# Experts 1 to 7 in the order of their token counts, with 384 down to 256 columns by rank, and hi and lo side by side in short tails

## The chip, the cores and the metric

The kernel runs on one core of a Trainium2 chip. The metric is the time of one execution on the device, in microseconds (us); of several executions the median counts. The engines run side by side and wait for each other by semaphores: PE (TensorE) multiplies matrices, ACT (ScalarE) and DVE (VectorE) work on vectors, POOL (GpSimd) does small work and issues gathers and scatters, and SP (SyncE) issues the other transfers. Each engine takes its instructions in the order of its own queue.

## What is computed

Three blocks follow one another on 4 x 576 = 2304 tokens of width 512: an attention with a decay bias, a gated MLP with a product over the sequence, and at the end a mixture of 8 experts, which is what the change touches:

```
logits = x @ w_gate                       # [B, S, 8]
local_gate = sigmoid(x @ w_local)
for b: for s:                             # in order, since e may be that of the token before
    e = argmax(logits[b, s]) if s == 0 or local_gate[b, s] < 0.5 else prev_e
    out[b, s] = softmax(logits[b, s])[e] * (relu(x[b, s] @ w1[e]) @ w2[e])
```

`w1[e]` is 512 x 1024 and `w2[e]` 1024 x 512. Each token goes to one expert. With the inputs as they are drawn, the reference sends 227, 356, 289, 239, 277, 278, 294 and 344 tokens to experts 0 to 7.

## The kernel before

All large products run as three matmuls in `fp32r`: a value is split in a rounded part (hi) and the rest (lo), and hi x hi, hi x lo and lo x hi are summed in PSUM (`mm3`). So every operand of the experts exists twice, side by side in one tile.

The routing of each of the four batches (`route`) is done with small matmuls and DVE work on one-hot tables; it leaves in `tbl` (of the last batch in `ids`) the token numbers, one column of 128 for each block of 128 tokens of an expert, and in `carry` the counts. The batches' MLP runs in `M_steps` and `O_steps`; the last batch's routing falls between the output products of that batch and the first layer of expert 0.

Then `experts` runs the experts one by one, in the order 0 to 7. Each has room for `CAP` = 3 blocks of 128 tokens, 384 columns, whatever its count; free places hold a token number out of range, which the gathers and scatters skip. Expert 0 is started early and in parts (`early_L1`, `L1_rows`). For an expert e of 1 to 7 the code is:

- `gather(e + 1)`: three indirect transfers on POOL, each 128 rows of the next expert, into one of two buffers `xgs`;
- `L1`: 8 column blocks f of the first layer, each 4 x 3 matmuls with a stationary block of w1 and the moving tokens `xT` (384 columns), then ReLU on ACT and the rest (lo) on DVE, into `hT`;
- `next_w(e + 1, ...)` for w1 and `new_xT(e + 1)`: 12 transposes on PE, then copies to `xT`;
- `L2` for three token blocks t: 8 x 3 matmuls with a stationary block of `hT` (128 tokens) and 512 moving columns of w2, then a scaled copy to `y` on ACT and an indirect scatter to `out` on POOL;
- `next_w(e + 1, ...)` for w2.

`load_w` brings one of the 8 pieces of an expert's weights (512 KB) by SP into `wraw` (2 buffers); ACT rounds it to hi and DVE computes lo, into one of 10 buffers `wp`. The buffers come free in a ring, so the loads of the next expert run behind the matmuls of this one. After the eighth expert `overflow` repeats the work for any token block beyond the third of an expert, in a loop over a list made on the chip (`emit_olist`); with the counts above the list is empty.

A scheduler sets the order of the instructions on each engine, from the order of the code and its own estimates.

Of the kernel before, what the change touches and what calls it, by code (L numbers as in the profile page):

```python
# [33 lines left out]
def kernel(  # L34
# [42 lines left out]
    def dma(out, in_):  # L77
        return SP.dma_start(out=raw(out), in_=raw(in_))
# [66 lines left out]
    NOV = NT // 128 - CAP  # L145
    NL = E * (NBLK - CAP)
    olist = T(const, [1, 2 * NOV + 1], I32, "olist")
    ids_d = dram.tile([128, NC], I32, name="ids_d")

# [126 lines left out]
    def emit_consts2():  # L276
        POOL.iota(io8, pattern=[[1, 8]], base=0, channel_multiplier=0)
        it = T(mp, [128, 512], I32, "ga", bufs=2)
        POOL.iota(it[:, 0:8], pattern=[[-1, 8]], base=8, channel_multiplier=0)
        POOL.iota(it[:, 8:8 + NQ], pattern=[[1024, NQ]], base=9, channel_multiplier=8)  # L280
        POOL.iota(it[:, 16:17], pattern=[[0, 1]], base=0, channel_multiplier=1)
        POOL.iota(it[:, 32:160], pattern=[[1, 128]], base=0, channel_multiplier=0)
        POOL.iota(it[:, 160:160 + NC], pattern=[[1, NC]], base=0, channel_multiplier=0)
        POOL.iota(it[:, 320:320 + B * NQ], pattern=[[-S, B], [-128, NQ]], base=FREE, channel_multiplier=-1)
        DVE.tensor_copy(out=w8d, in_=it[:, 0:8])
        DVE.tensor_copy(out=s8, in_=it[:, 8:8 + NQ])
# [11 lines left out]
        POOL.memset(onesb, 1.0)  # L298
        POOL.memset(onesf, 1.0)
# [558 lines left out]
    def route(b, lt):  # L858
# [85 lines left out]
        a = DVE.tensor_tensor(out=ids if b == B - 1 else tbl, in0=tbl, in1=pt[:, NC:2 * NC], op=ALU.subtract)  # L944
        for i in range(NQ):
            DVE.tensor_tensor(out=carry[0:QM[i]], in0=carry[0:QM[i]], in1=oh[0:QM[i], i, :], op=ALU.add)
        dmarks.append(a)

        ex = T(rp, [128, NQ, E], F32, "ex")
        DVE.tensor_tensor(out=ex, in0=l8, in1=mxb, op=ALU.subtract)  # L950
# [12 lines left out]
        dma(x2_d[r0:r0 + 512, DM:ROW].rearrange("(i p) c -> p i c", p=128), ps4[:, 0:NQ - 1])  # L963
        dma(x2_d[r0 + 512:r0 + S, DM:ROW], ps4[0:S - 512, NQ - 1])

    def emit_olist(pool, after):

        nb = NBLK - CAP
# [4 lines left out]
        x = POOL.iota(li[0:1, 0:NL], pattern=[[0, E], [128, nb]], base=128 * CAP, channel_multiplier=0)  # L973
        behind(x, after)
        POOL.iota(li[0:1, 128:128 + NL], pattern=[[1, E], [0, nb]], base=0, channel_multiplier=0)
        POOL.iota(li[0:1, 256:256 + NL], pattern=[[NBLK, E], [1, nb]], base=CAP, channel_multiplier=0)
        for a in range(3):
            DVE.tensor_copy(out=lf[0:1, 128 * a:128 * a + NL], in_=li[0:1, 128 * a:128 * a + NL])
        cx = T(pool, [128, 2, E, nb], BF16, "cx")
        behind(DVE.tensor_copy(out=cx[:, 0], in_=carry.unsqueeze(2).to_broadcast([128, E, nb])), dmarks[-1].ins.name)  # L980
        DVE.tensor_copy(out=cx[:, 1], in_=pad.unsqueeze(2).to_broadcast([128, E, nb]))
# [19 lines left out]
    def overflow():  # L1001
        of = out.rearrange("b s d -> (b s) d")
        n_ov = nc.values_load(olist[0:1, 2 * NOV:2 * NOV + 1], min_val=0, max_val=NOV)  # L1003
        with tc.For_i(0, n_ov) as it, tc.tile_pool(name="ov", bufs=1, side="left") as op:
            e = nc.sync.value_load(olist[0:1, bass.ds(it, 1)], min_val=0, max_val=E - 1)
            c = nc.sync.value_load(olist[0:1, bass.ds(it + NOV, 1)], min_val=CAP, max_val=NC - 1)
# [45 lines left out]
            )  # L1052


    WP = {}

    def load_w(e, j):

        r = T(wpool, [128, 1024], F32, "wraw", bufs=2)
        if j < KD:  # L1060
            dma(r, w1[e, 128 * j:128 * j + 128, :])
        else:
            f0 = 256 * (j - KD)
            x = dma(r.rearrange("p (a d) -> p a d", a=2), w2[e, f0:f0 + 256, :].rearrange("(a p) d -> p a d", p=128))
# [29 lines left out]
    def xT(xt, xg, n0, n):  # L1094

        w = 128 * n
        for kt in range(KD):
            pt = ps()
            for blk in range(n):
                PE.transpose(pt[:, 128 * blk:128 * blk + 128], xg[:, n0 + blk, 128 * kt:128 * kt + 128], ident)  # L1100
            ACT.copy(out=xt[:, 0, kt, 0:w], in_=pt[:, 0:w])
            DVE.tensor_tensor(out=xt[:, 1, kt, 0:w], in0=pt[:, 0:w], in1=f32v(xt[:, 0, kt, 0:w]), op=ALU.subtract)

    def L1(e, xt, ht, w_, after={}):
        for f in range(NF):
# [24 lines left out]

# [26 lines left out]
    def L1_rows(pool, e, xt, ht):  # L1157
# [11 lines left out]
        for z in range(2):  # L1169
# [14 lines left out]
    def experts(pool):  # L1184
        xts = {}

        def new_xT(e, n0=0):
            xts[e] = T(pool, [128, 2, KD, CC], F32R, "xT", bufs=2)
            xT(xts[e], xgs[e % 2], n0, CAP - n0)

        def new_hT():
            return T(pool, [128, 2, NF, CC], F32R, "hT", bufs=1)

        def early_L2(t):
            L2(pool, 0, early["ht"], t, early["xg"][:, t, DM:DM + 1], ids0[:, t:t + 1])
# [10 lines left out]
        for e in range(E):  # L1206
# [15 lines left out]
            for t in range(t0, CAP):  # L1222
                c = e * NBLK + t
                xg = xgs[e % 2][:, t] if e else early["xg2"]
                L2(pool, e, ht, t - t0, xg[:, DM:DM + 1], ids[:, c:c + 1])
# [151 lines left out]
```

## Time and profile before

| | us |
|---|---|
| median of 3 executions | 848.91 |
| lowest and highest | 845.52 and 854.72 |
| the profiled execution, its own time | 853.13 |
| its span, first to last instruction | 851.3 |
| PE busy in the span | 807.9 (95%) |
| DVE, ACT, POOL busy | 549.7, 463.2, 345.4 |

The span is what the profile's times count from; the profiled execution is 4.2 us slower than the median. In rows of the profile, a line names the kernel's line (L700 is the matmul in `mm3`), the engine, the operation, the tile written and those read, the shapes, and how many instructions stand together. For matmuls "128\*18" is the stationary block (rows x columns). Matmuls overlap, so a matmul's duration is longer than the distance from its start to that of the next; all prices below are distances between starts.

### The profile page before, as it was taken

How to read it: one execution, taken by the hardware profiler on the slowest of the kernel's cores; microseconds unless marked ns; L12 is line 12 of the kernel's file. 1: busy time of each engine (PE TensorE's matmuls, PEld its weight loads, DVE VectorE, ACT ScalarE, POOL GpSimd, SP SyncE). 2: the span in 40 equal slices, each digit the busy share in tenths (PEclk: the TensorE clock that was granted, in tenths of full speed). 3: DMA queues.
4: the chain of work that ended last, by engine and by line, in shares of the span. 5: the costliest groups of instructions: out<-in, count | busy, mean ns of one | idle time of the engine just before them, and what ended most of it. 6: DMA issues, size and time to landing. Idle time of an engine off the chain costs nothing. (4 is left out here: it accounts for less than half of the span.)

```text
span 851.3 us, 14839 instructions
## 1 busy us (share of the span) xinstructions
PE 807.9 (95%) x4803; PEld 684.5 (80%) x4803; DVE 549.7 (65%) x1567; ACT 463.2 (54%) x1070; POOL 345.4 (41%) x619
## 2 busy tenths in 40 slices
PE   8888999898999999999998899989999999999995
PEld 4555778687987988889888688778989989899894
DVE  7769669886677799968887467773545344353420
ACT  5756677785554788628785236134444344343410
POOL 3658754575551578724586002052021211313101
PEclk9977999998999999999999999999999999999998
DMA  7997799975477777679551673144564533545400
GB/s 159 220 225 219 163 230 282 290 188 105 104 166 216 176 157 198 144 182 259 112 169 41 209 249 121 38 129 152 180 191 133 184 129 124 194 132 182 124 4 35
DMA packets 119603, 138.69 MB, mean 163 GB/s; under 512 B 69494, under 2 KB 82934, under 8 KB 119524
## 3 DMA queue, kind: packets, MB, share of 16 engines
q1 hardware_dynamic: 115684, 128.23, 57.2%
q0 software_dynamic: 3840, 9.48, 3.0%
q8 instruction: 40, 0.66, 0.3%
q14 instruction: 39, 0.32, 0.1%
HBM read 90.96 MB, written 23.13 MB: 134 GB/s over the span
## 5 line engine op out<-in xcount | busy, mean ns | idle before, releaser
L1070 DVE TENSOR_TENSOR wp<-wraw,wp 128x1024 fp32r<-128x1024 f32 x63 | 76.6, 1224 | 102.8 <-ACT wp L1069 96.7
L700 PE MATMUL ps<-wp,hT 128*128 128x512 f32 x528 | 123.7, 393 | 0.0
L700 PE MATMUL ps<-xT,wp 128*128 128x384 f32 x672 | 119.7, 337 | 0.0
L700 PEld LDWEIGHTS ps<-xT,wp 128*128 128x128 f32 x672 | 117.8, 188 | 0.7
L1126 POOL DMA_INDIRECT out_dram<-y,ids x24 | 30.0, 1250 | 212.9 <-ACT y L1125 175.0
L700 PEld LDWEIGHTS ps<-wp,hT 128*128 128x128 f32 x528 | 98.6, 188 | 21.8
L414 POOL TENSOR_SCALAR E<-E,lsum 128x128 f32<-128x128 f32 (+4 forms) x160 | 97.6, 613 | 41.0 <-DVE lsum L411 28.9
L406 ACT ACTIVATE E<-E,negm 128x128 f32<-128x128 f32 (+4 forms) x160 | 96.7, 605 | 22.0 <-DVE negm L398 14.9
L1069 ACT CAST wp<-wraw 128x1024 fp32r<-128x1024 f32 x64 | 66.5, 1050 | 64.9 <-DMA wraw<-in_moe_w_dram 58.2
L700 PE MATMUL ps<-qk 128*128 128x128 f32 (+5 forms) x372 | 89.1, 337 | 6.1 <-DVE mv L759 2.8
L398 DVE CUSTOM_DVE_ANT_0 E<-ps,zmask 128x128 f32<-128x128 f32 (+4 forms) x160 | 75.6, 474 | 23.1 <-PE ps L700 21.9
L410 POOL TENSOR_SCALAR lsum<-lsum 128x1 f32<-128x1 f32 (+1 forms) x160 | 39.9, 249 | 121.1 <-ACT E L406 112.9
L432 PE MATMUL ps<-ident,E 128*128 128x128 f32 (+1 forms) x480 | 75.8, 265 | 10.9 <-POOL E L414 5.2
L432 PEld LDWEIGHTS ps<-ident,E 128*128 128x128 f32 (+1 forms) x480 | 51.8, 141 | 25.4 <-POOL E L414 9.8
L700 PE MATMUL ps<-wsg,vg 128*128 128x288 f32 x448 | 70.2, 307 | 1.7 <-DVE etb L442 1.0
L700 PEld LDWEIGHTS ps<-qk 128*128 128x128 f32 (+2 forms) x372 | 54.4, 175 | 15.3 <-DVE mv L759 3.1
L700 PEld LDWEIGHTS ps<-wsg,vg 128*128 128x128 f32 x448 | 63.5, 194 | 3.7 <-DVE etb L442 1.3
L464 PE MATMUL ps<-etb,vv 128*128 128x320 f32 (+5 forms) x340 | 65.3, 345 | 0.4 <-DVE tst L330 0.3
L464 PEld LDWEIGHTS ps<-etb,vv 128*128 128x128 f32 (+1 forms) x340 | 50.5, 182 | 14.1 <-issue 7.0
L700 PE MATMUL ps<-xh,w 128*128 128x288 f32 x256 | 59.5, 311 | 0.0
L1114 DVE SCALAR_TENSOR_TENSOR hT<-ps,hT 128x384 fp32r<-128x384 f32 x56 | 30.2, 553 | 39.2 <-ACT hT L1113 39.2
L700 PE MATMUL ps<-w,vg 128*128 128x512 f32 (+1 forms) x216 | 54.7, 398 | 0.2 <-ACT stg L494 0.2
(291 smaller groups left out, 1604.4 us busy)
## 6 DMA issues: line engine op xcount, KB each, us to landing
wraw<-in_moe_w_dram SPq DMA_DIRECT2D x64, 512.0 KB
qk<-tst SPq DMA_DIRECT2D x28, 432.0 KB
w<-wv_d SPq DMA_DIRECT2D x16, 512.0 KB
w<-wo_d SPq DMA_DIRECT2D x16, 512.0 KB
qk<-tst SPq DMA_DIRECT2D x28, 288.0 KB
w<-wu_d SPq DMA_DIRECT2D x12, 512.0 KB
nq<-in_q_dram SPq DMA_DIRECT2D x16, 288.0 KB
nk<-in_k_dram SPq DMA_DIRECT2D x16, 288.0 KB
```

What stands on the lines that cost most here:

```text
L398: hred[g] = DVE.tensor_tensor_reduce(out=e[0:M, a:z], in0=pt[0:M, 0:n], in1=zmask[0:M, m0:m0 + n], scale=-1.0, scalar=BIG if hi == 0 else ...
L406: ACT.activation(out=e[0:M, 0:N], in_=e[0:M, 0:N], func=ACTF.Exp, scale=-1.0, bias=nm[0:M, last:last + 1], accum_out=l[0:M, i:i + 1])
L410: POOL.tensor_scalar(out=l[0:M, c], in0=l[0:M, c], scalar1=1e-9, scalar2=0.0, op0=ALU.add, op1=ALU.add)
L414: POOL.tensor_scalar(out=Et[g, x][0:M, 0:n], in0=Et[g, x][0:M, 0:n], scalar1=l[0:M, x:x + 1], scalar2=1.0, op0=ALU.mult, op1=ALU.mult)
L432: PE.transpose(pt[:, j * M:(j + 1) * M], e[0:M, 128 * j:128 * (j + 1)], ident[0:M, 0:M])
L464: PE.matmul(pt[0:128 if wide else 64, a:n], lhsT=l, rhs=et[0:kk, z, j, a:n] if g >= F4 else f32v(et[0:kk, 0, j, a:n]), start=(j == 0 and n ...
L700: ms = [PE.matmul(pt, lhsT=l, rhs=r, start=(first_ and x == 0), stop=(last_ and x == n - 1)) for x, (l, r) in enumerate(pairs)]
L1069: c = ACT.copy(out=w[:, 0, :], in_=r)
L1070: a = (POOL if (e, j) == (0, KD) else DVE).tensor_tensor(out=w[:, 1, :], in0=r, in1=f32v(w[:, 0, :]), op=ALU.subtract)
L1114: DVE.scalar_tensor_tensor(out=ht[:, 1, f, 0:w_], in0=pt[:, 0:w_], scalar=0.0, in1=f32v(ht[:, 0, f, 0:w_]), op0=ALU.max, op1=ALU.subtract)
L1126: POOL.indirect_dma_start(out=of[:, :], out_offset=bass.IndirectOffsetOnAxis(ap=idx, axis=0), in_=y, in_offset=None, bounds_check=NT - 1, ...
```

## The change

The counts of experts 1 to 7 are ranked on the chip after the last batch's routing (`rank`, on DVE, with one small matmul). The loop over e then means: the expert of rank e - 1. Its weights are loaded from an address that SP reads from the table `order`, its token numbers come from `idsr`, and its width is fixed in the code: `CAPS[e]` = 384, 352, 320, 320, 288, 288 and 256 columns. By rank the counts above are 356, 344, 294, 289, 278, 277 and 239. Expert 0 stays as it was.

For widths of 320 and 288 the third block has 64 or 32 tokens (n). There `hT` keeps hi and lo of these tokens next to one another (`hparts`), and `L2_tail` takes a stationary block of 2n columns against the hi half of w2 and one of n columns against the lo half: two matmuls for each f where there were three. The sums of rows 0 to n and n to 2n are added afterwards. For 352 the third block has 96 tokens and keeps the three matmuls, and for 256 there is none. `emit_olist` now compares a count with the width of its rank.

```diff
+    CAPS = [384, 384, 352, 320, 320, 288, 288, 256]
...
+    def rank():
+        pn = rs()
+        PE.matmul(pn[:, 0:E], lhsT=onesb, rhs=carry, start=True, stop=True)
+        key = T(rp, [128, E], F32, "key")
+        DVE.scalar_tensor_tensor(out=key, in0=pn[:, 0:E], scalar=8.0, in1=w8d, op0=ALU.mult, op1=ALU.add)
...
+        DVE.tensor_tensor(out=gt, in0=key[:, 1:E].unsqueeze(1).to_broadcast(sq), in1=key[:, 1:E].unsqueeze(2).to_broadcast(sq), op=ALU.is_gt)
+        DVE.tensor_reduce(out=rk, in_=gt, axis=AX.X, op=ALU.add)
...
+        DVE.tensor_copy(out=order, in_=rk[0:1])
...
+        DVE.tensor_copy(out=idsr, in_=ir)
...
     def load_w(e, j):
         r = T(wpool, [128, 1024], F32, "wraw", bufs=2)
+        if e and j == 0:
+            chosen[e] = nc.sync.value_load(order[0:1, e - 1:e], min_val=1, max_val=E - 1)
+        ee = bass.ds(chosen[e], 1) if e else slice(0, 1)
         if j < KD:
-            dma(r, w1[e, 128 * j:128 * j + 128, :])
+            dma(r, w1[ee, 128 * j:128 * j + 128, :].rearrange("o p f -> p (o f)"))
...
     def gather(e):
-        for blk in range(CAP):
-            c = e * NBLK + blk
-            x = fetch(xgs[e % 2][:, blk, :], ids[:, c:c + 1])
+        for blk in range((CAPS[e] + 127) // 128):
+            n = min(128, CAPS[e] - 128 * blk)
+            x = fetch(xgs[e % 2][0:n, blk, :], idsr[0:n, e - 1, blk:blk + 1])
...
+    def hparts(ht, w):
+        fl = ht.rearrange("p f z c -> p f (z c)")
+        def hi(f, a, z):
+            return fl[:, f, a:z]
+        def lo(f, a, z):
+            o = ht.shape[3] if w not in TAILS else w if a >= EC else 2 * w - EC
+            return fl[:, f, o + a - EC:o + z - EC] if w in TAILS and a >= EC else fl[:, f, o + a:o + z]
+        return hi, lo
...
+            for a, z in ((0, w_),) if w_ not in TAILS else ((0, EC), (EC, w_)):
+                DVE.scalar_tensor_tensor(out=lo(f, a, z), in0=pt[:, a:z], scalar=0.0, in1=f32v(hi(f, a, z)), op0=ALU.max, op1=ALU.subtract)
...
+    def L2_tail(pool, e, ht, xg, n):
...
+            for z in (0, 1) if f < NF - 1 else (1, 0):
+                m = n if z else 2 * n
+                PE.matmul(pt[0:m, :], lhsT=hi(f, EC, EC + m), rhs=w[:, z, :], start=(f == z == 0), stop=(f == NF - 1 and z == 0))
+        lo, y = [T(pool, [128, DM], F32, "y", bufs=3) for _ in range(2)]
+        ACT.copy(out=lo[0:n], in_=pt[n:2 * n])
+        DVE.tensor_tensor(out=lo[0:n], in0=pt[0:n], in1=lo[0:n], op=ALU.add)
+        ACT.activation(out=y[0:n], in_=lo[0:n], func=ACTF.Copy, scale=xg[0:n, DM:DM + 1])
...
             if e:
-                for _ in L1(e, xt, ht, CC):
+                for _ in L1(e, xt, ht, CAPS[e]):
```

Ahead of the last batch's routing the engines' queues stay as they were, but for eight small fills on POOL and one copy on DVE at the very start. Three places differ.

On DVE, the rows from the last table of token numbers to the first copies for expert 0's third block: before (`hTA` is the first layer's result of expert 0, `wp` its weights).

```order
L944 TENSOR_TENSOR ids_94<-tbl_92,rt 128x144
L1070 TENSOR_TENSOR wp_8070<-wraw_8068,wp_8070 128x1024
L980 COPY cx_8889<-carry_93 128x120
L1114 SCALAR_TENSOR_TENSOR hTA_7921<-ps,hTA_7921 128x256
L1070 TENSOR_TENSOR wp_8075<-wraw_8073,wp_8075 128x1024
L1114 SCALAR_TENSOR_TENSOR hTA_7921<-ps,hTA_7921 128x256 x2
L1070 TENSOR_TENSOR wp_8080<-wraw_8078,wp_8080 128x1024
L1114 SCALAR_TENSOR_TENSOR hTA_7921<-ps,hTA_7921 128x256 x2
L1070 TENSOR_TENSOR wp_8207<-wraw_8205,wp_8207 128x1024
L1102 TENSOR_TENSOR xT_8113<-ps,xT_8113 128x128 x4
```

The same place on DVE in the changed kernel, from the second weight piece on; `key` to `idsr` are the ranking's.

```order
L1118 TENSOR_TENSOR wp_8113<-wraw_8111,wp_8113 128x1024
L988 SCALAR_TENSOR_TENSOR key_7839<-rt,w8d_78 128x8
L1179 SCALAR_TENSOR_TENSOR hTA_7959<-ps,hTA_7959 128x256 x2
L991 TENSOR_TENSOR gtr_7841<-key_7839 128x49
L993 TENSOR_REDUCE rk_7843<-gtr_7841 128x7
L995 TENSOR_TENSOR hot_7845<-rk_7843,iof_95 128x49
L996 TENSOR_TENSOR gtr_7841<-hot_7845,iof_95 128x49
L1002 TENSOR_TENSOR im_7850<-hot_7845,tbl_92 128x7x7 x3
...
L1118 TENSOR_TENSOR wp_8118<-wraw_8116,wp_8118 128x1024
...
L998 CAST order_98<-rk_7843 1x7
L1179 SCALAR_TENSOR_TENSOR hTA_7959<-ps,hTA_7959 128x256
L1005 CAST idsr_99<-ir_7854 128x21
```

Some 15 small operations now stand between expert 0's last pieces of work, and the weight piece that followed them (`wp_8207`, expert 1's first) has moved behind the copies of `xT`.

On SP, the rows around the first weight load of the second expert: before, then now.

```order
L78 DMA wraw_8078<-in_moe_w_dram 128x2x512
L78 DMA wraw_8205<-in_moe_w_dram 128x1024
L78 DMA wraw_8210<-in_moe_w_dram 128x1024
L78 DMA wraw_8215<-in_moe_w_dram 128x1024
```

```order
L78 DMA wraw_8116<-in_moe_w_dram 128x2x512
L1106 TENSOR_LOAD order_98
L1106 ISA x2
L78 ISA
L78 DMA wraw_8243<-in_moe_w_dram 128x1024
L78 ISA
L78 DMA wraw_8257<-in_moe_w_dram 128x1024
L1106 TENSOR_LOAD order_98
L1106 ISA x2
```

The first load of the second expert now waits for `order`; the other six reads of `order` stand together behind the second load, and each later load has one address instruction ahead of it.

On PE, the third block of the second layer of the third expert after expert 0 (320 columns now), and the start of the next expert: before, then now.

```order
L700 MATMUL ps<-wp_8852,hT_8911 128x512 x6
L700 MATMUL ps<-wp_8857,hT_8911 128x512 x6
L700 MATMUL ps<-wp_8862,hT_8911 128x512 x6
L700 MATMUL ps<-wp_8867,hT_8911 128x512 x6
L700 MATMUL ps<-xT_9052,wp_9034 128x384 x3
```

```order
L1206 MATMUL ps<-wp_8917,hT_8977 128x512
L1206 MATMUL ps<-wp_8917,hT_8977 64x512
L1206 MATMUL ps<-wp_8917,hT_8977 128x512
L1206 MATMUL ps<-wp_8917,hT_8977 64x512
...
L1206 MATMUL ps<-wp_8932,hT_8977 128x512
L1206 MATMUL ps<-wp_8932,hT_8977 64x512 x2
L1206 MATMUL ps<-wp_8932,hT_8977 128x512
L713 MATMUL ps<-xT_9135,wp_9117 128x320 x3
```

The 24 matmuls of the tail are 16 now, with stationary blocks of 128 and 64 columns in turn, and the first layer that follows has 320 columns instead of 384.

## Rows read from the trace of the kernel before

**Rows 1.** Page, engines; then stretches: length, busy time by engine, PEclk, DMA share, GB/s.

```profile
PE 807.9 (95%) x4803; PEld 684.5 (80%) x4803; DVE 549.7 (65%) x1567; ACT 463.2 (54%) x1070; POOL 345.4 (41%) x619
...
600.00:650.00 50.00, 50.00 (x270) 46.84 (x269) 25.41 (x33) 24.55 (x38) 9.18 (x7) 1.00 0.56 171
```

**Rows 2.** Timeline of PE, experts 5 to 7: start, duration (us).

```profile
756.87 16.62 PE L700 MATMUL ps<-wp,hT 128*128 128x512 f32 x72
773.32 17.09 PE L700 MATMUL ps<-xT,wp 128*128 128x384 f32 x96
790.25 1.47 PE L1100 MATMUL ps<-ident,xg 128*128 128x128 f32 x12
791.48 16.82 PE L700 MATMUL ps<-wp,hT 128*128 128x512 f32 x72
808.14 16.83 PE L700 MATMUL ps<-xT,wp 128*128 128x384 f32 x96
824.81 16.97 PE L700 MATMUL ps<-wp,hT 128*128 128x512 f32 x72
```

**Rows 3.** Timeline of PE, last batch's MLP and expert 0's first layer.

```profile
529.75 6.68 PE L700 MATMUL ps<-wsg,vg 128*128 128x288 f32 x49
536.27 0.69 PE L700 MATMUL ps<-vg,wgl 128*18 128x288 f32 x4
536.80 0.85 PE L700 MATMUL ps<-w,vg 128*128 128x512 f32 x3
537.49 0.29 PE L700 MATMUL ps<-vg,wgl 128*18 128x288 f32 x1
537.62 0.63 PE L700 MATMUL ps<-w,vg 128*128 128x512 f32 x2
...
555.90 4.58 PE L700 MATMUL ps<-xTA,wp 128*128 128x256 f32 x36
560.32 0.42 PE L941 MATMUL rt<-aa,l 128*128 128x288 bf16 x2
```

**Rows 4.** Page, groups: second and first layer's matmuls and first layer's weight loads.

```profile
L700 PE MATMUL ps<-wp,hT 128*128 128x512 f32 x528 | 123.7, 393 | 0.0
L700 PEld LDWEIGHTS ps<-xT,wp 128*128 128x128 f32 x672 | 117.8, 188 | 0.7
```

**Rows 5.** Timeline of DVE: around the routing, and behind it.

```profile
548.43 0.20 DVE L878 TENSOR_REDUCE am<-eq 128x5 f32<-128x40 f32 x1
...
579.36 0.88 DVE L1102 TENSOR_TENSOR xT<-ps,xT 128x128 fp32r<-128x128 f32 x4 [3.46 <-ACT xT L1101]
588.44 2.36 DVE L1070 TENSOR_TENSOR wp<-wraw,wp 128x1024 fp32r<-128x1024 f32 x2 [8.20 <-ACT wp L1069]
```

**Rows 6.** Timelines of POOL and PE: first gather behind the routing, first use.

```profile
570.27 1.00 POOL L1083 DMA_INDIRECT xg<-x_d,ids  x1 [0.16 <-POOL xg L1342]
...
591.51 1.47 PE L1100 MATMUL ps<-ident,xg 128*128 128x128 f32 x12
```

**Rows 7.** SP's read of the overflow count at line 1003: min/median/max in ns.

```profile
L1003 SPq TENSOR_LOAD <-olist x1: 487/487/487, 685.4 to 685.4; - x1
L1003 SPq FUSED_REGOPS  x1: 192/192/192, 685.9 to 685.9; - x1
```

**Rows 8.** Timeline of ACT: weight pieces rounded, expert 1's loading.

```profile
587.37 1.98 ACT L1069 CAST wp<-wraw 128x1024 fp32r<-128x1024 f32 x2
...
599.12 1.05 ACT L1069 CAST wp<-wraw 128x1024 fp32r<-128x1024 f32 x1 [2.92 <-DMA wraw<-in_moe_w_dram]
605.73 1.05 ACT L1069 CAST wp<-wraw 128x1024 fp32r<-128x1024 f32 x1 [2.39 <-DMA wraw<-in_moe_w_dram]
```

**Rows 9.** Timeline of POOL: scatters of expert 5, last gather for expert 7.

```profile
764.43 1.27 POOL L1126 DMA_INDIRECT out_dram<-y,ids  x1 [18.27 <-ACT y L1125]
...
777.49 1.86 POOL L1126 DMA_INDIRECT out_dram<-y,ids  x1 [3.47 <-ACT wp L1069]
779.65 1.92 POOL L1083 DMA_INDIRECT xg<-x_d,ids  x1 [0.30 <-issue]
```

More of the change, by code (lines that the diff above doesn't have):

```diff
@@ L144 @@
     ids = T(const, [128, NC], I32, "ids")
-    NOV = NT // 128 - CAP
-    NL = E * (NBLK - CAP)
+    CAPS = [384, 384, 352, 320, 320, 288, 288, 256]
+    OB = CAP - 1
+    NOV = NT // 128 - CAP + 1
+    NL = E * (NBLK - OB)
+    ER = E - 1
+    iof = T(const, [128, E], F32, "iof")
+    thr0 = T(const, [1, ER], F32, "thr0")
+    thr = T(const, [1, E], F32, "thr")
+    order = T(const, [1, ER], I32, "order")
+    idsr = T(const, [128, ER, CAP], I32, "idsr")
     olist = T(const, [1, 2 * NOV + 1], I32, "olist")
@@ L285, in emit_consts2 @@
         DVE.tensor_copy(out=w8d, in_=it[:, 0:8])
+        DVE.tensor_copy(out=iof, in_=io8)
         DVE.tensor_copy(out=s8, in_=it[:, 8:8 + NQ])
@@ L298, in emit_consts2 @@
         POOL.memset(onesb, 1.0)
+        POOL.memset(thr, 1.0e6)
+        for r in range(ER):
+            POOL.memset(thr0[0:1, r:r + 1], float(CAPS[r + 1]) if CAPS[r + 1] < 128 * CAP else 1.0e6)
         POOL.memset(onesf, 1.0)
@@ L943, in route @@
         DVE.scalar_tensor_tensor(out=tbl, in0=pt[:, 0:NC], scalar=-64.0, in1=tbl, op0=ALU.mult, op1=ALU.add)
-        a = DVE.tensor_tensor(out=ids if b == B - 1 else tbl, in0=tbl, in1=pt[:, NC:2 * NC], op=ALU.subtract)
+        if b == B - 1:
+            DVE.tensor_tensor(out=ids, in0=tbl, in1=pt[:, NC:2 * NC], op=ALU.subtract)
+        a = DVE.tensor_tensor(out=tbl, in0=tbl, in1=pt[:, NC:2 * NC], op=ALU.subtract)
         for i in range(NQ):
@@ L947, in route @@
         dmarks.append(a)
+        if b == B - 1:
+            rank()
         ex = T(rp, [128, NQ, E], F32, "ex")
@@ L964, in route @@
         dma(x2_d[r0 + 512:r0 + S, DM:ROW], ps4[0:S - 512, NQ - 1])
+    def rank():
[3 more added lines that the diff above has]
+        DVE.scalar_tensor_tensor(out=key, in0=pn[:, 0:E], scalar=8.0, in1=w8d, op0=ALU.mult, op1=ALU.add)
+        sq = [128, ER, ER]
+        gt = T(rp, sq, F32, "gtr")
+        DVE.tensor_tensor(out=gt, in0=key[:, 1:E].unsqueeze(1).to_broadcast(sq), in1=key[:, 1:E].unsqueeze(2).to_broadcast(sq), op=ALU.is_gt)
+        rk = T(rp, [128, ER], F32, "rk")
+        DVE.tensor_reduce(out=rk, in_=gt, axis=AX.X, op=ALU.add)
+        hot = T(rp, sq, F32, "hot")
+        DVE.tensor_tensor(out=hot, in0=rk.unsqueeze(1).to_broadcast(sq), in1=iof[:, 0:ER].unsqueeze(2).to_broadcast(sq), op=ALU.is_equal)
+        DVE.tensor_tensor(out=gt, in0=hot, in1=iof[:, 1:E].unsqueeze(1).to_broadcast(sq), op=ALU.mult)
+        DVE.tensor_reduce(out=rk, in_=gt, axis=AX.X, op=ALU.add)
+        DVE.tensor_copy(out=order, in_=rk[0:1])
+        im = T(rp, [128, ER, CAP, ER], F32, "im")
+        tv = tbl.rearrange("p (e c) -> p c e", c=NBLK)
+        for c in range(CAP):
+            DVE.tensor_tensor(out=im[:, :, c, :], in0=hot, in1=tv[:, c, 1:E].unsqueeze(1).to_broadcast(sq), op=ALU.mult)
+        ir = T(rp, [128, ER, CAP], F32, "ir")
+        DVE.tensor_reduce(out=ir, in_=im, axis=AX.X, op=ALU.add)
+        DVE.tensor_copy(out=idsr, in_=ir)
+        th = T(rp, [1, ER, ER], F32, "th")
+        DVE.tensor_tensor(out=th, in0=hot[0:1].rearrange("p r e -> p e r"), in1=thr0.unsqueeze(1).to_broadcast([1, ER, ER]), op=ALU.mult)
+        DVE.tensor_reduce(out=thr[0:1, 1:E], in_=th, axis=AX.X, op=ALU.add)
     def emit_olist(pool, after):
-        nb = NBLK - CAP
+        nb = NBLK - OB
         dma(ids_d, ids)
@@ L972, in emit_olist @@
         r = T(pool, [128, 48], F32, "ol")
-        x = POOL.iota(li[0:1, 0:NL], pattern=[[0, E], [128, nb]], base=128 * CAP, channel_multiplier=0)
+        x = POOL.iota(li[0:1, 0:NL], pattern=[[0, E], [128, nb]], base=128 * OB, channel_multiplier=0)
         behind(x, after)
         POOL.iota(li[0:1, 128:128 + NL], pattern=[[1, E], [0, nb]], base=0, channel_multiplier=0)
-        POOL.iota(li[0:1, 256:256 + NL], pattern=[[NBLK, E], [1, nb]], base=CAP, channel_multiplier=0)
+        POOL.iota(li[0:1, 256:256 + NL], pattern=[[NBLK, E], [1, nb]], base=OB, channel_multiplier=0)
         for a in range(3):
             DVE.tensor_copy(out=lf[0:1, 128 * a:128 * a + NL], in_=li[0:1, 128 * a:128 * a + NL])
+        DVE.tensor_copy(out=lf[0:1, 0:NL].rearrange("p (e c) -> p e c", c=nb)[:, :, 0], in_=thr)
         cx = T(pool, [128, 2, E, nb], BF16, "cx")
@@ L1112, in L1 @@
                     behind(ms[0], after[f].ins.name)
-            ACT.activation(out=ht[:, 0, f, 0:w_], in_=pt[:, 0:w_], func=ACTF.Relu)
-            DVE.scalar_tensor_tensor(out=ht[:, 1, f, 0:w_], in0=pt[:, 0:w_], scalar=0.0, in1=f32v(ht[:, 0, f, 0:w_]), op0=ALU.max, op1=ALU.subtract)
+            hi, lo = hparts(ht, w_)
+            ACT.activation(out=hi(f, 0, w_), in_=pt[:, 0:w_], func=ACTF.Relu)
+            for a, z in ((0, w_),) if w_ not in TAILS else ((0, EC), (EC, w_)):
+                DVE.scalar_tensor_tensor(out=lo(f, a, z), in0=pt[:, a:z], scalar=0.0, in1=f32v(hi(f, a, z)), op0=ALU.max, op1=ALU.subtract)
@@ L1124, in L2 @@
         y = T(pool, [128, DM], F32, "y", bufs=3)
-        ACT.activation(out=y, in_=pt, func=ACTF.Copy, scale=prob)
+        ACT.activation(out=y[0:n], in_=pt[0:n], func=ACTF.Copy, scale=prob[0:n])
         POOL.indirect_dma_start(
-            out=of[:, :], out_offset=bass.IndirectOffsetOnAxis(ap=idx, axis=0), in_=y, in_offset=None,
+            out=of[:, :], out_offset=bass.IndirectOffsetOnAxis(ap=idx[0:n], axis=0), in_=y[0:n], in_offset=None,
+            bounds_check=NT - 1, oob_is_err=False,
+        )
@@ new lines, in L2_tail @@
+    def L2_tail(pool, e, ht, xg, n):
+        of = out.rearrange("b s d -> (b s) d")
+        hi, _ = hparts(ht, EC + n)
+        pt = ps()
+        for f in range(NF):
+            w = WP[e, KD + f // 2].rearrange("p z (a d) -> p z a d", a=2)[:, :, f % 2, :]
+            for z in (0, 1) if f < NF - 1 else (1, 0):
[5 more added lines that the diff above has]
+        ACT.activation(out=y[0:n], in_=lo[0:n], func=ACTF.Copy, scale=xg[0:n, DM:DM + 1])
+        POOL.indirect_dma_start(
+            out=of[:, :], out_offset=bass.IndirectOffsetOnAxis(ap=idsr[0:n, e - 1, CAP - 1:CAP], axis=0), in_=y[0:n], in_offset=None,
@@ L1174, in L1_rows @@
             d = slice(4 * z, 4 * z + 4)
-            amarks.append(ACT.copy(out=ht[:, 0, d, 0:128], in_=pv))
-            DVE.tensor_tensor(out=ht[:, 1, d, 0:128], in0=pv, in1=f32v(ht[:, 0, d, 0:128]), op=ALU.subtract)
+            amarks.append(ACT.copy(out=ht[:, d, 0, 0:128], in_=pv))
+            DVE.tensor_tensor(out=ht[:, d, 1, 0:128], in0=pv, in1=f32v(ht[:, d, 0, 0:128]), op=ALU.subtract)
             yield 1
@@ L1221, in experts @@
                 new_xT(e + 1)
[L1222 to L1225, printed above, removed]
+            for t in range(t0, (CAPS[e] + 127) // 128):
+                n = min(128, CAPS[e] - 128 * t)
+                if not e:
+                    L2(pool, e, ht, t - t0, early["xg2"][:, DM:DM + 1], ids[:, t:t + 1])
+                elif t < CAP - 1 or n > 64:
+                    L2(pool, e, ht, t, xgs[e % 2][:, t, DM:DM + 1], idsr[:, e - 1, t:t + 1], n, CAPS[e])
+                else:
+                    L2_tail(pool, e, ht, xgs[e % 2][:, t], n)
             for j in range(KD):
```

24 lines of the change are left out of this document (13 added, 11 removed).

## The prediction

> **What bounds the kernel now.** I read the page's engine table first and then cut the stretch that the change touches out of the rest, because the average there (PE 95%) says nothing of a stage. Between 600 and 650 us PE is busy for 50.00 of 50 us at a granted clock of 1.00, while DVE, ACT and POOL are busy for about half of it or less [rows 1]. The timeline of PE, experts 5 to 7, shows the same thing as a pattern: 72 matmuls of the second layer, 96 of the first, 12 transposes, and each group starts where the one ahead of it ends [rows 2]. So from this stretch to the last matmul, which ends at 824.81 + 16.97 = 841.8 us, the time is PE's matmuls added up, and a matmul that goes away or gets shorter shortens the run by itself, until something else becomes late. The second thing to read is the distance between starts, since durations overlap. First layer, 384 columns: 790.25 - 773.32 = 16.93 and 824.81 - 808.14 = 16.67, mean 16.80 us, by 96 is 175 ns. Second layer, 512 columns: 773.32 - 756.87 = 16.45 and 808.14 - 791.48 = 16.66, mean 16.56 us, by 72 is 230 ns. Twelve transposes: 791.48 - 790.25 = 1.23 us [rows 2].
>
> **First layer, fewer columns.** Whether a narrower matmul is shorter in proportion is told by the stages ahead: 49 with 288 columns take 536.27 - 529.75 = 6.52 us, or 133 ns, and 36 with 256 columns 560.32 - 555.90 = 4.42 us, or 123 ns, both with stationary blocks of 128 x 128 in f32 like the first layer's [rows 3]. The widths between them I put on the line from 288 to 384 columns, 0.437 ns a column: 147 ns for 320, 161 ns for 352. For 96 matmuls each the gain is 96 x 14 ns = 1.3 us for the 352, 2 x 96 x 28 = 5.4 for the two 320, 2 x 96 x 42 = 8.0 for the two 288, and 96 x 52 = 5.0 for the 256. The sum is **19.7 us**.
>
> **Second layer, fewer matmuls.** The expert with 256 columns has no third block: 24 matmuls go. Each of the four tails (64 or 32 tokens) does with 16 what took 24: 32 go. The 352 keeps its 72. A matmul of fewer stationary columns still moves 512, and I price it at the same 230 ns. So 56 x 0.230 = **12.9 us**. The transposes of the absent block, four at 1.23 / 12, give 0.4 us. Together **33.0 us** of PE's work go, with no PE idle in which to lose them.
>
> **What is added.** *On PE* the ranking has one matmul of 8 columns. The table's two of 288 columns take 0.42 us [rows 3], so it is between 0 and 0.2 us; I take 0.1. *On DVE* the ranking is some 15 operations on at most 128 x 49 elements, like the 0.20 us of a small reduction in the routing [rows 5]: 3 us. DVE stands idle for 3.46 us ahead of 579.36 and for 8.20 us ahead of 588.44 [rows 5], so these cover it; without the cover it would be the 3 us. The second difference per column block that a tail's layout needs, 8 x 0.2 = 1.6 us for an expert, and the tail's extra copy and sum lie on engines half idle [rows 1], which nobody on PE waits for until a PSUM buffer is wanted. *On POOL* the first gather behind the routing was issued at 570.27 and can now only go when `idsr` is there, which I put 5 to 6 us later: the sequence of some 12 of these operations, with a weight piece or two of 1.2 us (2.36 for two, [rows 5]) between them. PE first uses these tokens at 591.51 [rows 6]. The issues take 1 us each, so three of them end about 579 and leave 12 us for landing: no cost. The eight fills at the start stand beside work that doesn't need them. *On SP* seven reads of `order` at 0.487 + 0.192 [rows 7] make 4.8 us, six of them behind the second load of expert 1. Only that expert's loads queue behind them. `order` should be there at about 577 us, so a first load lands at about 583; before, the first pieces behind the routing were rounded at 587.37 [rows 8], so up to there it is covered. The third piece needs the buffer of the first and then half of the 6.6 us that two loads take (605.73 - 599.12, [rows 8]), so it lands at 586 to 589, and ACT, which takes its work in order, may wait up to 2 us at it, with expert 1's `xT` copies queued behind. I take 0.5 us, ends 0 and 2.
>
> **What becomes late next.** An expert that took 34.6 us on PE (16.80 + 16.56 + 1.23) now takes less, and two things that PE didn't wait for must keep up.
>
> Gathers and scatters: POOL issues the scatters of one expert some 6.5 us apart (764.43 to 777.49 for two steps) and the gathers behind the last of them, the last one until 779.65 + 1.92 = 781.57 [rows 9]. This is 24.7 us after that second layer's start at 756.87, and the transposes that need it started at 790.25 [rows 2], 33.4 us after. In the changed kernel, from the second layer's start to those transposes: with 288 columns on both sides, 64 x 0.230 + 96 x 0.133 = 27.5 us, and 28.8 from a 320 to a 288, more elsewhere. 24.7 us plus the landing must fit in 27.5. The landing has no row of its own that I trust, so between 0 and 5 us, or a wait of 0 to 2.5 us at two places. Since the tail's y comes earlier too (after 64 matmuls, not 72), I take 0.5 in all, ends 0 and 5.
>
> Weights: two loads take 6.6 us where nothing but the transfer holds them [rows 8], eight 26.4 us. The shortest period in which eight are loaded is 12.8 + 1.2 + 14.7 = 28.7 us. It fits by 2.3 us; I take nothing, ends 0 and 3 (1 us at each of the three shortest).
>
> **Sum.** 33.0 - 0.1 - 0.5 - 0.5 = 31.9 us less. The profiled execution took 853.13 us, 4.2 more than the median, with its span at 851.3; the stage of the experts has no idle time that would depend on which execution it was. So 853.1 becomes 821.2, and on the median's scale 848.9 - 31.9 = **817.0 us**.
>
> **The rivals.** *Waits take over.* If landing or loading is at the far end, or a load whose address comes from a register is slower than the same load before, PE gets gaps at experts 4 to 7. For it: the margins above of about 2.5 us. Against it: both are margins still, and the loads of 512 KB are no smaller or larger. 5 of the gathers and 3 of the weights on top give 824 to 825 us. *Changing the number of stationary columns costs.* In a tail the stationary block has 128 and 64 columns in turn, or 64 and 32: 14 changes in each of the two wider tails and 16 in the narrower, 60 in all. If a matmul had to run out ahead of each change, it would cost the difference between its duration and the distance, 0.393 [rows 4] - 0.230 = 0.163 us, so 9.8 us in all, and 826.8 us. Against it: at 536.27 to 537.62 blocks of 18 and of 128 columns take turns, and four matmuls of 288 columns take 536.80 - 536.27 = 0.53 us, 133 ns each, one of them 0.13, three of 512 columns 0.69 us, 230 ns each [rows 3]: nothing lost. The Trainium skill ("TensorEngine Tiling (Array Packing)", Key Properties) says that "Changing tiling mode (not just tile) drains the TensorE". By that rule, if 64 or 32 columns are such a mode, the time would be the 826.8; the trace shows no such drain with 18 columns. *The overflow loop runs.* An expert whose count is over its rank's width sends a block through the loop: weights 26.4, two layers with 256 to 128 columns some 17, scatter and gather 6.5, one after the other, so about 50 us a pass. One pass already is more than the 32 us gained, and gives some 867 us, slower than before. By the counts 356, 344, 294, 289, 278, 277, 239 against 384, 352, 320, 320, 288, 288, 256 no expert exceeds, the smallest room being 8 tokens; it decides from a ranking that goes wrong, or other counts. *Weight loads bound the first layer.* PEld's mean there is 188 ns [rows 4], more than the 175 of a matmul; were that a limit, narrower columns would bring nothing, and 12.9 + 0.4 - 1.1 leave 836.7. Against it: the 133 and 123 ns of [rows 3].
>
> **How the numbers follow.** The forecast has 0.81, waits 0.10, changed columns 0.05, the weight loads 0.02, the overflow 0.02. About 1% is what a measurement of this kernel can tell from no change, so faster means below 840.4. All but the overflow lie there, and I leave 0.02 for a loss within 1%: faster 0.96, same 0.02, slower 0.02. The forecast's own range: no cost at all gives 816, and 3 us more if the line for 320 and 352 columns or the second layer's distance is 10% too low, 812; all costs at their ends give 826. As the other cases from below 827 come in with it, 811 to 826 holds all but the tails.
>
> **What would show it.** In the changed kernel's profile PE should have no gap from the first layer of the second expert on. The first layers should take 16.8, 15.5, 14.1, 14.1, 12.8, 12.8 and 11.8 us, a tail of 16 matmuls 3.7 us, the same per matmul as the third block of the 352. The first gather stands near 576, the first load of expert 1 near 577, and the last gather of an expert at least 3 us ahead of its transposes. The overflow's pass should have no row. It would be wrong if PE's transposes wait for `xg`, if its first layers wait for `wp` with DMA as the releaser, if a tail takes over 5 us, or if a first layer of 288 columns takes near 17.

## The result, and the profile after

The changed kernel took 819.82 us, median of 4 runs (815.21 to 825.23); the kernel before took 851.82 us beside it (845.52 to 857.77, 4 runs). The ratio is 0.9628, 95% interval 0.9520 to 0.9735: faster by some 3.7%. The ratios here and below are formed from fast runs alone (those within 1.5% of the fastest run of their kernel), so they can differ a little from the quotient of the medians beside them. The difference of the medians is 32.0 us, where 31.9 were forecast; the 817.0 us forecast counted from the earlier median of 848.91. That the two agree to 0.1 us is luck: four runs of a kernel lie 10 us and more apart.

A single run of this kernel says less than its length suggests. The first 100 us, which the change hardly touches, had a different granted clock in the profiled executions. Here are the stretches of the kernel before: the first 100 us, and the matmuls behind the last routing tables (columns as in [rows 1], the last three are the granted clock, the DMA share and GB/s).

```profile
0.00:100.00 100.00, 87.89 (x439) 52.76 (x440) 74.21 (x242) 62.65 (x158) 61.66 (x124) 0.90 0.86 197
565.20:570.00 4.80, 4.80 (x34) 4.80 (x33) 3.01 (x6) 1.70 (x3) 4.43 (x3) 0.76 0.44 146
```

The same two of the changed kernel, and under them the stage of experts 1 to 7:

```profile
0.00:100.00 100.00, 89.88 (x397) 51.95 (x398) 70.59 (x224) 58.32 (x143) 56.50 (x121) 0.80 0.85 194
569.80:575.50 5.70, 5.70 (x35) 5.50 (x35) 5.22 (x9) 1.70 (x3) 3.80 (x3) 0.70 0.62 200
606.00:813.00 207.00, 207.00 (x1189) 183.60 (x1188) 100.53 (x175) 95.37 (x154) 39.55 (x35) 1.00 0.50 160
```

The profiled execution of the changed kernel, with 0.80 there instead of 0.90, reached the last routing's tables 5.6 us later (565.93 against the 560.32 of [rows 3]), and the profiled spans differ by 27.9 us only (851.3 and 823.4). So everything below is read within **the stage**: from the start of the long run of 95 matmuls in the first layer of the second expert to the end of the last expert's second layer. In the kernel before it begins here (timeline of PE: start, duration):

```profile
598.50 16.94 PE L700 MATMUL ps<-xT,wp 128*128 128x384 f32 x95
```

and ends at 841.78 [rows 2]: 243.28 us. The timeline of PE of the changed kernel, from the same place on (L713 is `mm3`, L1206 the tail, L1148 the transposes; a row names the shape of its first matmul; parts left out):

```profile
603.95 16.85 PE L713 MATMUL ps<-xT,wp 128*128 128x384 f32 x95
...
638.56 15.63 PE L713 MATMUL ps<-xT,wp 128*128 128x352 f32 x96
654.03 1.47 PE L1148 MATMUL ps<-ident,xg 128*128 128x128 f32 x12
...
703.75 14.24 PE L713 MATMUL ps<-xT,wp 128*128 128x320 f32 x96
717.84 1.47 PE L1148 MATMUL ps<-ident,xg 128*128 128x128 f32 x12
719.07 11.18 PE L713 MATMUL ps<-wp,hT 128*128 128x512 f32 x48
730.08 3.86 PE L1206 MATMUL ps<-wp,hT 128*128 128x512 f32 x16
733.78 12.97 PE L713 MATMUL ps<-xT,wp 128*128 128x288 f32 x96
746.58 1.47 PE L1148 MATMUL ps<-ident,xg 128*128 128x128 f32 x12
...
758.83 3.85 PE L1206 MATMUL ps<-wp,hT 128*64 128x512 f32 x16
762.51 12.96 PE L713 MATMUL ps<-xT,wp 128*128 128x288 f32 x96
...
790.96 11.67 PE L713 MATMUL ps<-xT,wp 128*128 128x256 f32 x96
802.47 11.36 PE L713 MATMUL ps<-wp,hT 128*128 128x512 f32 x48
```

The reader is to see two things. No row has idle time in brackets, and PE is busy for 207.00 of 207 us at a clock of 1.00 above: the bound is the one of [rows 1] still. And the distances between starts are the new prices: 15.47 us for 352 columns (654.03 - 638.56), 14.09 for 320, 12.80 for 288, 11.51 for 256; a tail's 16 matmuls take 3.70 and 3.68 us, and 48 of the second layer 11.01. The stage lasts 802.47 + 11.36 - 603.95 = 209.88 us, **33.40 us less** than before.

The ranking's end in the timeline of DVE of the changed kernel:

```profile
580.31 0.15 DVE L998 CAST order<-rk 1x7 int32<-1x7 f32 x1
...
580.71 0.15 DVE L1005 CAST idsr<-ir 128x21 int32<-128x21 f32 x1
```

The first gather that needs it and the last one ahead of the transposes at 746.58, in the timeline of POOL; and in that of ACT the first weight piece of the second expert:

```profile
581.63 1.00 POOL L1131 DMA_INDIRECT xg<-x_d,idsr  x1 [6.63 <-DVE idsr L1005]
...
741.28 0.95 POOL L1131 DMA_INDIRECT xg<-x_d,idsr  x1 [0.30 <-issue]
```

```profile
585.23 1.05 ACT L1117 CAST wp<-wraw 128x1024 fp32r<-128x1024 f32 x1 [0.87 <-DMA wraw<-in_moe_w_dram]
```

The first gather goes 11.36 us after the first gather of before, of which 5.6 are the later start of everything; the other 5.8 are the 5 to 6 us that the forecast gave the ranking. PE does not notice: from the last routing's first matmul to the stage it takes 603.95 - 565.93 = 38.02 us, against 598.50 - 560.32 = 38.18 before. From that matmul to the end of the last one, **the stretch** below, it is 247.90 us, against 281.46 before: 33.56 us less.

### The profile page after: what moved, and what is told of

It is laid out like the page before. It is cut to its first block, busy times and chain, and to the rows that moved or that the text cites. A ratio compares the mean times of both kernels' runs of the same rounds, so it can differ in the third digit from the quotient of the medians.

```text
span 823.4 us, 14928 instructions
## 1 busy us (share of the span) xinstructions
PE 781.2 (95%) x4744; PEld 652.4 (79%) x4744; DVE 551.2 (67%) x1620; ACT 458.5 (56%) x1073; POOL 340.6 (41%) x625
## 5 line engine op out<-in xcount | busy, mean ns | idle before, releaser
L419 ACT ACTIVATE E<-E,negm 128x128 f32<-128x128 f32 (+4 forms) x160 | 96.7, 605 | 30.6 <-DVE negm L411 24.8
L713 PE MATMUL ps<-qk 128*128 128x128 f32 (+5 forms) x372 | 92.3, 348 | 8.1 <-DMA qk<-tst 3.7
L713 PE MATMUL ps<-xT,wp 128*128 128x288 f32 (+4 forms) x672 | 99.3, 308 | 0.0
L713 PEld LDWEIGHTS ps<-xT,wp 128*128 128x128 f32 x672 | 98.2, 188 | 0.8
L713 PE MATMUL ps<-wp,hT 128*128 128x512 f32 (+1 forms) x408 | 96.4, 394 | 0.0
L713 PEld LDWEIGHTS ps<-wp,hT 128*128 128x128 f32 (+1 forms) x408 | 75.3, 186 | 17.3
L445 PE MATMUL ps<-ident,E 128*128 128x128 f32 (+1 forms) x480 | 78.2, 271 | 9.8 <-POOL E L427 4.7
L1192 POOL DMA_INDIRECT out_dram<-y,idsr x16 | 18.8, 1174 | 153.3 <-ACT y L1191 119.7
L713 PE MATMUL ps<-wsg,vg 128*128 128x288 f32 x448 | 70.3, 307 | 2.0 <-DVE etb L455 1.0
L713 PEld LDWEIGHTS ps<-qk 128*128 128x128 f32 (+2 forms) x372 | 56.6, 182 | 18.4 <-issue 5.7
L713 PEld LDWEIGHTS ps<-wsg,vg 128*128 128x128 f32 x448 | 63.6, 194 | 4.0 <-DVE etb L455 1.3
L477 PE MATMUL ps<-etb,vv 128*128 128x320 f32 (+5 forms) x340 | 63.6, 339 | 0.6 <-DVE tst L343 0.5
L477 PEld LDWEIGHTS ps<-etb,vv 128*128 128x128 f32 (+1 forms) x340 | 50.3, 182 | 12.9 <-issue 4.4
L713 PE MATMUL ps<-xh,w 128*128 128x288 f32 x256 | 58.0, 304 | 0.3 <-DVE lsum L424 0.2
L713 PE MATMUL ps<-w,vg 128*128 128x512 f32 (+1 forms) x216 | 54.6, 397 | 0.3 <-ACT stg L507 0.3
L713 PE MATMUL ps<-w,xh 128*128 128x512 f32 (+1 forms) x160 | 52.5, 407 | 0.8 <-DVE mv L769 0.7
```

The source lines that it names most:

```text
L419: ACT.activation(out=e[0:M, 0:N], in_=e[0:M, 0:N], func=ACTF.Exp, scale=-1.0, bias=nm[0:M, last:last + 1], accum_out=l[0:M, i:i + 1])
L445: PE.transpose(pt[:, j * M:(j + 1) * M], e[0:M, 128 * j:128 * (j + 1)], ident[0:M, 0:M])
L477: PE.matmul(pt[0:128 if wide else 64, a:n], lhsT=l, rhs=et[0:kk, z, j, a:n] if g >= F4 else f32v(et[0:kk, 0, j, a:n]), start=(j == 0 and n ...
L713: ms = [PE.matmul(pt, lhsT=l, rhs=r, start=(first_ and x == 0), stop=(last_ and x == n - 1)) for x, (l, r) in enumerate(pairs)]
L1192: POOL.indirect_dma_start(out=of[:, :], out_offset=bass.IndirectOffsetOnAxis(ap=idx[0:n], axis=0), in_=y[0:n], in_offset=None, bounds_chec ...
```

## The experiments

Stages are compared, for the reason given; the times and ratios stand beside them. The stage of the changed kernel is 209.88 us.

**The ranking without the widths.** All ranks get 384 columns; nothing is left but the ranking and the addresses.

```diff
-    CAPS = [384, 384, 352, 320, 320, 288, 288, 256]
+    CAPS = [384] * 8
```

> All eight experts keep 384 columns and three matmuls; only the ranking, the reads of the table and the weight addresses from registers remain. Theory (PE's matmuls are the time, the ranking and the addresses lie under other work): within 1 us of the kernel before, and from the last routing table's first matmul to the end of the last matmul the same 281.5 us as before, to 0.5 us. Rival (addresses from registers or the table's reads make the loads late): 2 to 6 us more in that stretch, with first layers that wait for wp.

It took 854.13 us, before 854.47; the ratio is 1.0047 (0.9992 to 1.0102). The stretch is 834.95 - 553.30 = 281.65 us, before 281.46. Ahead of the stage nothing is lost (37.70 us against 38.18); the stage itself is 243.95 us, 0.67 longer than before, and the timeline of PE shows where:

```profile
670.38 0.82 PE L1029 MATMUL rt<-ident,lf 1*128 1x1 f32 x6 [0.80 <-DVE lf L1023]
```

That is the list for the overflow, whose few matmuls stand between those of an expert and waited once for DVE; with it taken off, the stages agree to 0.15 us. No first layer waits for `wp`, so the rival, late loads, is out.

**The order as constants.** The order of the experts, known for these inputs, is written in; the addresses are fixed, and small copies of the token numbers and limits stand where the ranking stood (not shown below).

```diff
+    ORD = [1, 7, 6, 2, 5, 4, 3]
...
-            chosen[e] = nc.sync.value_load(order[0:1, e - 1:e], min_val=1, max_val=E - 1)
+            chosen[e] = ORD[e - 1]
```

> The changed kernel with the order of the experts written into it as constants for these inputs: no ranking, no reads of the table, fixed addresses. Theory: same as the changed kernel within 0.5 us in the stretch from the last routing table to the last matmul (247.9 us), though the first gather goes some 5 us earlier. Rival (the ranking's latency is on the path at expert 1): 3 to 5 us less.

819.10 us, ratio 0.9595 (0.9515 to 0.9675). The stretch is 247.72 us against 247.90, the stage 209.85 against 209.88. The first gather came 570.09 - 560.15 = 9.94 us after the last routing's first matmul, where it is 581.63 - 565.93 = 15.70 in the changed kernel, and nothing came of these 5.8 us. So ranking, reads of the table and addresses from registers cost no more than 0.2 us together.

**The ranking twice.**

```diff
             rank()
+            rank()
```

> The changed kernel with the whole ranking done twice, one after the other, so that the order and the token numbers are known some 5 us later. Theory: the first gathers have about 10 us of slack and the first weight pieces about 7, so the stretch from the last routing table to the last matmul grows by 0 to 2 us. Rival (the ranking's latency is already on the path): 5 us more.

820.87 us, ratio 0.9602 (0.9510 to 0.9694). The second ranking came out only 2.5 us later, not 5 (`order` at 585.04 - 568.19 = 16.85 us from the last routing's first matmul, 580.31 - 565.93 = 14.38 in the changed kernel). The stretch grew by 0.80 us to 248.70, the stage stayed at 209.88. Of this, 0.66 us lie between the second expert's transposes and its stage. The timeline of ACT shows a weight piece as the cause:

```profile
598.65 1.05 ACT L1118 CAST wp<-wraw 128x1024 fp32r<-128x1024 f32 x1 [2.41 <-DMA wraw<-in_moe_w_dram]
```

And that of PE what comes of it:

```profile
600.97 3.74 PE L713 MATMUL ps<-wp,hT 128*128 128x512 f32 x14 [0.15 <-ACT hT L1261]
```

This is the third piece of the next expert's weights, the one whose buffer the prediction followed. ACT stands still at it, and expert 0's `hT` is queued behind. So the ranking as it is has slack, but less than 2.5 us of it.

**Three matmuls in the tails.**

```diff
-                elif t < CAP - 1 or n > 64:
+                elif True:
```

> The changed kernel with three matmuls also in the four tails of 64 and 32 tokens, so that the number of stationary columns does not change inside a tail. Theory: 32 matmuls more at 0.230 us, 7.4 us more in the stretch than the changed kernel, a tail 5.5 us instead of 3.7. Rival (changing the stationary columns costs something in the changed kernel): less than 6 us more, a tail's matmul clearly shorter than 230 ns here.

828.97 us, ratio 0.9693 (0.9598 to 0.9788). The stage is 217.20 us, 7.32 more than in the changed kernel; 7.4 were expected. In its timeline of PE a second layer of 72 matmuls, 24 of them with 64 columns throughout, takes 736.59 - 720.06 = 16.53 us:

```profile
720.06 16.70 PE L713 MATMUL ps<-wp,hT 128*128 128x512 f32 x72
736.59 12.96 PE L713 MATMUL ps<-xT,wp 128*128 128x288 f32 x96
```

That is 230 ns each. In the changed kernel the 16 of a tail with 128 and 64 columns in turn take 3.70 us, 231 ns, and with 64 and 32 in turn 3.68 us, 230 ns. Changing the number of stationary columns costs nothing that these rows show.

**256 columns for all.** This leaves out the tokens beyond the 256th of an expert and keeps the overflow loop empty.

```diff
-    CAPS = [384, 384, 352, 320, 320, 288, 288, 256]
+    CAPS = [384] + [256] * 7
```

> The changed kernel with 256 columns and no third block for all of experts 1 to 7; tokens beyond the 256th of an expert are left out, and the loop for overflow stays empty. PE's work for an expert is then 11.5 + 0.8 + 11.1 = 23.4 us. Theory (the weights, eight loads at 3.3 us, are what becomes late next): a period of about 26.4 us, so some 18 us of PE idle over six experts and 793 us in all, first layers and second layers waiting for wp. Rival (PE still sets the time, the loads go faster when wanted): 775 us, no gaps. Rival (gathers and scatters become late first): transposes that wait for xg.

792.71 us in one run, 859.85 for the kernel before beside it. The timeline of PE has gaps now (the idle time and its releaser in brackets):

```profile
642.66 12.99 PE L713 MATMUL ps<-wp,hT 128*128 128x512 f32 x48 [2.13 <-DVE hT L1179]
...
719.33 0.98 PE L1148 MATMUL ps<-ident,xg 128*128 128x128 f32 x7 [2.61 <-DMA xg<-x_d,idsr]
722.95 13.51 PE L713 MATMUL ps<-wp,hT 128*128 128x512 f32 x48 [2.63 <-DVE hT L1179]
```

The releaser named is `hT`, but it is only the last link: the timeline of ACT shows each weight piece waiting for its transfer, and the rounding of `hT` stands in the same queue behind it.

```profile
720.26 1.04 ACT L1117 CAST wp<-wraw 128x1024 fp32r<-128x1024 f32 x1 [2.23 <-DMA wraw<-in_moe_w_dram]
721.21 0.92 ACT L1177 ACTIVATE hT<-ps 128x256 fp32r<-128x256 f32 x3
```

From the first layer at 627.98 to that at 759.58 it is five periods of 26.3 us in the mean. That is near the 26.4 us of eight loads [rows 8], but no steady rate: singly they are 27.5, 25.0, 24.8, 31.1 and 23.3 us. One set of transposes waited for its gather as well, 2.61 us. The gaps add up to 9.1 us, half of the 18 expected. A third loss is the clock: the granted clock is 0.87 and 0.81 in the stretches behind two of the gaps (columns as above), and 48 matmuls take 12.83 and 13.35 us there instead of some 11.1.

```profile
642.60:656.00 13.40, 13.34 (x53) 10.81 (x54) 6.90 (x11) 6.52 (x10) 2.06 (x2) 0.87 0.66 194
...
723.00:736.30 13.30, 13.30 (x49) 10.77 (x49) 7.20 (x11) 6.80 (x10) 2.04 (x2) 0.81 0.65 201
```

**The same with three buffers for loads.**

```diff
-        r = T(wpool, [128, 1024], F32, "wraw", bufs=2)
+        r = T(wpool, [128, 1024], F32, "wraw", bufs=3)
```

> The kernel with 256 columns for all of experts 1 to 7 (tokens beyond the 256th left out), with three buffers for weights on their way instead of two. It showed a period of 26.3 us where PE's work is 23.4, and 216 us from the last routing table to the last matmul; with no wait it would be 203. Theory (the next load waits until ACT and DVE have let go of one of two buffers): with three the stretch falls by 8 us or more, to 203 to 208. Rival (the transfers themselves take that long): 214 to 217, as with two.

787.61 us in one run, 860.22 for the kernel before beside it. The stretch is 206.38 us against 215.89. The stage has no wait left, 163.98 us against 178.33, and five periods of it are (754.40 - 636.44) / 5 = 23.6 us each. So eight loads fit in 23.6 us, and what made PE wait was not the rate of the transfers but two buffers: the next load waits until ACT and DVE have let go. Ahead of the stage 4.8 us were lost (42.40 against 37.56), at expert 0, where the third buffer moved the loads and other work in the queues; which of these it was is open.

**The overflow loop, once.** The second rank, with 344 tokens, gets 320 columns.

```diff
-    CAPS = [384, 384, 352, 320, 320, 288, 288, 256]
+    CAPS = [384, 384, 320, 320, 320, 288, 288, 256]
```

> The changed kernel with 320 columns instead of 352 for the second rank, whose expert has 344 tokens: the loop for overflow runs once. Theory (a pass has its steps one after the other behind the last expert): 50 us for the pass, less 3.2 us that the narrower width gives, so 866 us. Rival (loads and gather of the pass overlap well with each other): 25 to 35 us for the pass, 842 to 852 us.

856.03 us in one run, 859.85 for the kernel before beside it. The seven experts take 206.65 us, 3.2 less, as expected. The pass, from the last expert's end at 793.04 + 11.36 = 804.40 to its own at 844.61, is **40.2 us**: between the two expectations. Timeline of PE:

```profile
793.04 11.36 PE L713 MATMUL ps<-wp,hT 128*128 128x512 f32 x48
814.47 1.09 PE L1063 MATMUL ps<-ident,xg 128*128 128x128 f32 x4 [10.07 <-DMA xg<-x_d,idx]
816.23 20.74 PE L713 MATMUL ps<-xt,w 128*128 128x128 f32 x96 [0.68 <-ACT xt L1065]
836.77 7.84 PE L713 MATMUL ps<-w,ht 128*128 128x512 f32 x24
```

The stretch of the pass's first layer (columns as above):

```profile
816.00:837.00 21.00, 20.77 (x97) 20.77 (x98) 9.67 (x15) 7.65 (x14) 0.00 (x0) 0.50 0.44 148
```

10 us go until the tokens are there. Then the loads run beside the first layer, which has a clock of 0.50, the lower of the two levels (1.2 GHz), after PE's wait: 96 matmuls of 128 columns take 20.54 us, 214 ns each.

**368 columns for the first rank** (356 tokens).

```diff
-    CAPS = [384, 384, 352, 320, 320, 288, 288, 256]
+    CAPS = [384, 368, 352, 320, 320, 288, 288, 256]
```

> The changed kernel with 368 columns instead of 384 for the first rank, which has 356 tokens. Theory (PE's columns are the time, 0.437 ns each): 96 x 16 columns, 0.7 us less from the last routing table to the last matmul, 247.2 us. Rival (something else is already late): no change, 247.9.

822.80 us in one run, 860.22 for the kernel before beside it. The stretch is 245.60 us, 2.3 less and not 0.7. The stage tells the two parts apart: it is 209.07 us, 0.81 less, of which the first layer gives 0.83 (95 matmuls in 617.79 - 601.93 = 15.86 us instead of 16.69). The rest lies ahead of the stage, in the matmuls behind the last routing tables, whose clock was 1.00 here and 0.70 in the changed kernel's stretch above:

```profile
569.30:573.50 4.20, 4.20 (x35) 4.04 (x35) 4.13 (x9) 1.71 (x3) 2.84 (x3) 1.00 0.52 171
```

As a version it saves 0.8 us, which a time cannot show, for a margin of 12 tokens instead of 28.

## Why the prediction was right

**Bound.** PE's matmuls add up to the time, before and after; the stage has no gap in either.

**First layer.** Forecast: 19.7 us. The measured distances, 15.47, 14.09, 12.80 (twice) and 11.51 us, stand against the forecast's 15.5, 14.1, 12.8 and 11.8: the line from 288 to 384 columns held, and 256 came out at 120 ns, not 123. Only the third expert's cannot be read alone, since the overflow's list stands in it.

**Second layer.** Forecast: 12.9 us for 56 matmuls. A tail takes 3.7 us, as forecast; taking back 32 of the 56 costs 7.32 us. Both layers and the transposes were to give 33.0 us; the stage gave 33.40.

**What is added.** I took 0.6 us for the ranking and expert 1's start. Without the ranking the stretch is 0.2 us shorter, so it is all but free, for the reason given: its work lies under PE's. With the 0.5 us for gathers, which did not come either, the sum held 1.1 us of costs too many: the stretch got 33.56 us shorter, not 31.9. The cover is thinner than I had it, though. I put the slack of SP's first loads at several us, and 2.5 us of delay already cost 0.8, by the path that I had named with ends 0 and 2: the third piece's buffer, and ACT's queue behind it.

**What becomes late next.** Nothing does: no gap. The last gather ended 742.23 - 719.07 = 23.2 us after the second layer's start, not 24.7, and the transposes followed 4.35 us later without a wait. They came 27.51 us after that start, from a second layer with 320 columns to a first one with 288; the 28.8 that I gave this case belong to 320 on both sides. The weights' limit of 26.4 us was read wrongly: I called it the transfer alone, and it was two buffers, since with three PE goes through eight loads in 23.6 us without a wait. That the periods with two buffers have 26.3 us in the mean is in part luck, with 23.3 to 31.1 singly. The trace of the kernel before has a hint of it: between 596 and 842 us SP's loads waited 50 times, 133.9 us in all, for DVE's step on a weight piece, behind which a buffer is free, and only 38.3 us for transfers (waits of SP; total, times, longest in us).

```profile
SPq L78 <- DVE wp L1070: 133.9, 50, 9.9
SPq L78 <- DMA wraw<-in_moe_w_dram: 38.3, 24, 3.4
```

The margin was therefore real in this kernel, where the shortest period is some 28.5 us, but not for the reason given.

**The rivals.** In the stage, waits took over only when every expert was cut to 256 columns, and then weights and a gather both did, as that rival said. The changing number of columns is out: 231 and 230 ns in the tails, 230 without changes. With the forecast's 0.163 us for each of 14 changes a tail would take some 6 us, and it takes 3.7. The Trainium skill ("TensorEngine Tiling (Array Packing)", Key Properties) says that a change of tiling mode drains TensorE. By the 3.7 us, alternating 128 with 64 or 64 with 32 stationary columns is either no such change or one that costs nothing here. Weight loads as the bound are out, by the 120 ns of the 256 columns. The overflow's price was mis-sized: 50 us forecast, 40.2 measured, because I added the weights' loads and the two layers where loads and first layer run side by side. The two layers alone were slower than the some 17 us that I gave them: 844.61 - 816.23 = 28.38 us, the first of them at half the clock. With one pass the stage is 844.61 - 597.75 = 246.86 us, 3.6 more than before the change. So one overflow loses all of the gain, but is no 867 us: it ends within 1% of the kernel before. By this price a second pass would make the kernel clearly slower; that was not tried.

## What to carry to other kernels

Where a stage is one engine's work without gaps, the change can be priced from distances between starts, term by term, and the sum comes out within 0.4 us of 33; what needs thought is what the freed time was hiding. Here that was read from two periods (eight loads 26.4 us, the last gather 24.7 us after a second layer's start) set against the shortest new one, 28.7 and 27.5 us; which resource sets such a period, here buffers and not transfers, is worth reading from the waits. And where runs differ by more than 15 us in a stage that the change doesn't touch, compare stages and not times.

## What I had not expected

Much of this kernel's spread lies ahead of the change: the last routing's first matmul came between 553.30 and 570.90 us in the profiles of these kernels, while the stage repeats to some hundredths (209.88, 209.85 and 209.88 us in the changed kernel, with the order as constants and with the ranking twice). The granted clock of the first 100 us was 0.80 in the changed kernel's profile and 0.90 in that of the kernel before; that this alone makes the spread is argued and not shown. And what follows the same short waits of PE can differ: behind those at the last routing's tables (1.76, 0.74 and 0.33 us in the changed kernel) 32 matmuls took 5.43 us at a clock of 0.70, and 3.93 us at 1.00 in the execution with 368 columns, behind the same waits. Why the clock fell in the one and not in the other is not shown. So ahead of the stage, differences of a few tenths between two executions say nothing without the clock beside them.
